# Two transformer layers on one Trainium2 core: attention values issued in the same stretch as a score visit

## The chip, the core and the metric

The kernel runs on one core of a Trainium2 chip. The metric is device time in microseconds (us) of one execution; a run is given as the median over several executions. The names of the engines are those of the profile: PE is TensorE (matmul), PEld its weight loads, ACT is ScalarE, DVE is VectorE, POOL is GpSimd, SP is SyncE, which here only issues DMA transfers.

## What is computed

Two layers, one after the other, each an attention block and a gated MLP, both on the normalized residual stream. The second layer has the same weights.

```python
x = A_x                                   # 1 x 2048 x 512, bf16
for _ in range(2):
    x = x + attention(layernorm(x))       # 32 heads of 16, each query sees itself and the 255 keys before it
    x = x + mlp(layernorm(x))             # (sigmoid(x Wg) * (x Wu)) Wd, hidden width 1792
# attention: softmax(q k^T / 4, masked) v, then Wo; q, k, v = x Wqkv
```

## The kernel before

The 2048 rows are 16 tiles of 128 (`t`), in four groups of four (`g`); `L` is the layer. All engines' programs are written by a planner that runs while the program is built: the class `Plan` keeps an assumed clock for each engine, tasks for ACT, DVE, POOL and SP enter queues with a priority (a lower number goes first), and `pick` (from line 1024) decides what PE gets next whenever the assumed PE is free. What comes out is a fixed order of instructions for each engine, with semaphores between them. So the times in the planner (such as `EXP_NS = 1880`) order the instructions, and the chip then runs that order as fast as its waits allow.

PE's work has three kinds. The planner calls them modes, since the array is used in three shapes:

- "d", full 128x128 matmuls: units for q, k and v (L572, L601, L637), gate and up (L662), down (L695), output projection (L723), a few transposes through PE (L532, L999), and matmuls on the identity that fill empty time in the first 85 us of the plan (L1108, `keep_warm`). Each unit writes one of four PSUM banks (`bank`), and the bank is given back when ACT or DVE has copied it out.
- "s", score visits (L853, L863, L873): 24 to 32 small matmuls in strips of 32 rows that fill the tile `Sps`, which takes four PSUM banks and exists once. After each visit ACT makes one exponential of 128x2048 (L905) into the ring `PTring` or into `edge`, and only then may the next visit overwrite `Sps`. A tile has five visits (one "R", four "A"), the last tile of a layer two; that is 154 visits. A visit is due when `PACE` has passed since the one before (2700 ns in the first layer, 3000 ns in the second) and its exponential is planned to be over.
- "pv", values (L932): for each half of the heads of a tile, 32 to 80 small matmuls in strips of 32 columns into one bank. They need the exponentials and the masks that DVE multiplies into them (L791), the values `Vaug` (copied out of PSUM by ACT or DVE, L553 or L555), and copies of every second row of them, `Vl` and `Vh`, which SP's DMA makes (L1131). There are 64.

After the values: the bank is copied to `OTs` by ACT (L553) or DVE (L555), whichever is planned to be done first; then a DMA transpose to `Oq` (L951), the division by the softmax sum on DVE (`norm`, L986 and L987), a DMA transpose to `OnT` (L959), the output projection on PE, the sum and the layer norm on DVE and POOL (L729, L498 to L520), a DMA transpose to `xnT` (L544), gate and up for a tile or a pair of tiles, tanh on ACT (L674), the product into `hT` on DVE (L677), and the down projection (L695, L704).

In `pick`, `go` is the time until the exponential of the last visit is over, `wait` the longer of that and of what is left of the pace. In the kernel before, values that are ready go when the next visit is due within 600 ns (or when no visit is in sight, or when the last exponential has not begun):

```python
if pv and (wait <= 600 or wait > 1e8 or held):
    return self.do_values(pv, spare)
```

Of the kernel before, what the change touches and what calls it, by code (L numbers as in the profile page):

```python
# [15 lines left out]
NT = S // P  # L16
# [8 lines left out]
NBG = TGW // P  # L25
# [58 lines left out]
def dve_ns(n):  # L84
    return 152 + n / 0.96
# [43 lines left out]
def when_all(events, fn):  # L129
    left = [e for e in events if not e.fired]  # L130
    if not left:
        fn()
        return
    count = [len(left)]

    def one():
        count[0] -= 1
        if count[0] == 0:
            fn()

    for e in left:
        e.waiting.append(one)
# [152 lines left out]
def mm_ns(n):  # L295
    return n / 2.4 + 2.5


class Net:
# [74 lines left out]
    def loads(self, A_x, wqkv, wo, w_gate, w_up, w_down):  # L374
        nc, pl = self.nc, self.pl
        wq_src = wqkv.rearrange("(k p) m -> p k m", p=P)
        wo_src = wo.rearrange("(k p) m -> p k m", p=P)
        wd_src = w_down.rearrange("(c p) m -> p c m", p=P)
        wg_src = w_gate.rearrange("(k p) f -> p k f", p=P)
        wu_src = w_up.rearrange("(k p) f -> p k f", p=P)  # L380
        self.has_x, self.has_wq = {}, {}

        def load_x(dst, tiles, n, prio, queues=("SP", "SP"), after=0):
            done, parts = Event(), []
            for z in range(2):
                src = A_x[0].rearrange("(t z k) d -> z k t d", z=2, k=HP)[z][:, tiles, :]
                parts.append(load(dst[z:P:2], src, n * HP * D * 2, after, (), prio, queues[z]))
            when_all(parts, done.fire)
            return done

        def load(dst, src, nbytes, after=0, deps=(), prio=2, queue="SP"):
            ns = max(520, 40 + nbytes / 1024 * 0.95)
            q = {"SP": nc.sync, "ACT": nc.scalar}[queue]
            return pl.dma(ns, nbytes, lambda: q.dma_start(out=dst, in_=src), deps, prio, after, queue).done

        for t in range(0, NBG, 2):
            self.has_x[t] = self.has_x[t + 1] = load_x(self.xsb[:, t:t + 2, :], slice(t, t + 2), 2, 0, ("SP", "ACT"))
        for i, k in enumerate("kqv"):
            h = slice("qkv".index(k) * D, ("qkv".index(k) + 1) * D)
            self.has_wq[k] = load(self.wq[:, :, h], wq_src[:, :, h], D * D * 2, prio=0, queue="ACT" if i < 3 else "SP")  # L400

        def x_group(g, after):
            h = slice(g * NBG, (g + 1) * NBG)
            ev = load_x(self.xsb[:, h, :], h, NBG, 2 if g > 1 else 2, after=after)
            for t in range(g * NBG, (g + 1) * NBG):
                self.has_x[t] = ev

        x_group(1, 0)
        gap, at = 1300, 6000
        self.has_wo = load(self.wot[:], wo_src, D * D * 2, after=at)  # L410
        at += gap * 2
        n = F // 2
        gu = []
        for i in range(2):
            h = slice(i * n, (i + 1) * n)
            pair = []
            for w, src in ((self.wg, wg_src), (self.wu, wu_src)):
                pair.append(load(w[:, :, h], src[:, :, h], D * n * 2, after=at))
                at += gap * 7 // 2
            gu.append(pair)  # L420
            if i == 0:
                x_group(2, at)
                at += gap * 2
        self.has_gu = [gu[fc * 2 // FC] for fc in range(FC)]
        self.has_wd = Event()
        parts = []
        for i in range(0, FC, 2):
            h = slice(i, i + 2)
            parts.append(load(self.wd[:, h, :], wd_src[:, h, :], 2 * P * D * 2, after=at))
            at += gap  # L430
        when_all(parts, self.has_wd.fire)
        x_group(3, at)
# [257 lines left out]
    def down_unit(self, L, t, t0, n, chunks):  # L690
        nc, pl = self.nc, self.pl

        def mm(bank, fc):
            c, o = (chunks[fc], (t - t0) * P) if n == 2 else (chunks[fc // 2], fc % 2 * P)
            nc.tensor.matmul(self.banks[bank][:], lhsT=self.hT[:, c, o:o + P], rhs=self.wd[:, fc, :],  # L695
                             start=fc == 0, stop=fc == FC - 1)
            if t == t0 + n - 1:
                pl.at(pl.pe_free + PE_LATENCY, self.h_used[L, t0, fc].fire)

        def steps(bank):  # L700
            return [(mm_ns(D), lambda fc=fc: mm(bank, fc)) for fc in range(FC)]

        def evac(u):
            d = pl.task({"DVE": dve_ns(D)}, lambda e: nc.vector.scalar_tensor_tensor(  # L704
                out=self.xsb[:, t, :], in0=self.banks[u.bank][:], scalar=0.5, in1=self.xsb[:, t, :],
                op0=ALU.mult, op1=ALU.add), [u.done], 1)
            if L == 0:
                self.layer_norm(("p", 1, t // NBG), t, [d.done], 5)
            else:
                dst = self.out[0, t * P:(t + 1) * P, :].rearrange("(z k) d -> z k d", z=2)  # L710
                for z in range(2):
                    pl.dma(450, HP * D * 2, lambda z=z: nc.sync.dma_start(out=dst[z], in_=self.xsb[z:P:2, t, :]), [d.done])
            return d.done

        u = Unit(("d", L, t), steps, [self.has_wd] + ([] if t == t0 else [self.down_began[L, t - 1]]), False, evac)
        u.want = [self.h_ready[L, t0, fc] for fc in range(FC)]
        return u

    def oproj_unit(self, L, t, b):
        nc, pl = self.nc, self.pl  # L720

        def steps(bank):
            return [(mm_ns(D), lambda c=c: nc.tensor.matmul(  # L723
                self.banks[bank][:], lhsT=b[0][:, c, :], rhs=self.wot[:, c, :],
                start=c == 0, stop=c == KT - 1)) for c in range(KT)]

        def evac(u):
            u.done.then(lambda: self.give(b))
            d = pl.task({"DVE": dve_ns(D)}, lambda e: nc.vector.tensor_tensor(  # L729
                out=self.xsb[:, t, :], in0=self.xsb[:, t, :], in1=self.banks[u.bank][:], op=ALU.add), [u.done], 1)  # L730
            self.layer_norm(("g", L, t // NBG), t, [d.done], 0 if L * NT + t < 1 else 2)
            return d.done

        return Unit(("o", L, t), steps, [self.has_wo], False, evac)
# [203 lines left out]
    def after_values(self, L, t, half, bank, done):  # L938
        nc, pl = self.nc, self.pl
        box = self.outs.setdefault((L, t), {})  # L940
        early = L * NT + t < 1

        def move(e):
            if "OTs" not in box:
# [24 lines left out]
        b = pl.dma(1800, 262144, turn, [box[0], box[1]], 0 if early else 1)  # L969
        b.can = lambda: self.has("Oq")  # L970
        b.done.then(lambda: self.give(box["OTs"]))
        c = pl.task({"DVE": 960}, norm, [b.done], 0 if early else 3, lambda: self.has("On"), port=True)
        c.done.then(lambda: (self.give(box["Oq"]), self.give(box["Rt"])))
        d = pl.dma(1190, 131072, turn2, [c.done], 0 if early else 1)
        d.can = lambda: self.has("OnT")
# [53 lines left out]
    def pick(self):  # L1029

        pl = self.pl
        s = self.slot
        visit = None
        wait = 1e9
        if s < len(self.visits):
            if s == 0 or self.exps[s - 1].ends is not None:
                if all(e.fired for e in self.v_needs[s]):
                    wait = 0 if s == 0 or self.exps[s - 1].done.fired else self.exps[s - 1].ends - pl.now
                    visit = self.visits[s]
            elif all(e.fired for e in self.v_needs[s]):  # L1040
                wait = EXP_NS
        go = wait
        wait = max(wait, self.last_s + self.pace(s) - pl.now)
        pv = None
        spare = [i for i in range(BANKS) if self.bank_user[i] is None]
        if self.pv_list and spare:
            L, t, h = self.pv_list[0]
            if len(self.masks[L, t, h]) == self.n_masks(t) and all(e.fired for e in self.masks[L, t, h]) and all(
                    self.v_ready[L, jj].fired for jj in range(max(0, t - 2), t + 1)) and self.v_lo[L, t].fired and (
                    t < 2 or self.v_hi[L, t - 2].fired):  # L1050
                pv = self.pv_list[0]
        held = s < len(self.visits) and s > 0 and self.exps[s - 1].ends is None
        if pv and (wait <= 600 or wait > 1e8 or held):
            return self.do_values(pv, spare)
        u = None
        if wait >= 60:
# [1 line left out]
        if visit and (wait <= 0 or go <= 0 and u is None):  # L1058
# [4 lines left out]
            L, t = visit[:2]  # L1063
# [166 lines left out]
    def go(self, *srcs):  # L1230
        pl = self.pl
# [45 lines left out]
        c = 0  # L1277
        for L in range(2):
            t0 = 0
            while t0 < NT:  # L1280
                k = 1 if L * NT + t0 < 4 or L * NT + t0 >= 2 * NT - 0 else 2
                m = FC * k // 2
                chunks = [(c + i) % HCH for i in range(m)]
                c += m
                gs += [self.gate_up_unit(L, t0, k, (i,) if k == 2 else (2 * i, 2 * i + 1), chunks[i]) for i in range(m)]
                for t in range(t0, t0 + k):
                    d = self.down_unit(L, t, t0, k, chunks)
                    d.begin = self.down_began[L, t]
                    ds.append(d)
                t0 += k  # L1290
# [51 lines left out]
```

## Time and profile before

| | |
|---|---|
| median of 6 runs | 554.66 us (553.48 to 556.49) |
| the profiled execution | 554.57 us, of which the span from the first to the last instruction is 552.8 us |
| PE, PEld, ACT, DVE, POOL busy | 537.1, 353.8, 411.2, 397.9, 62.3 us |
| exponentials (L905 on ACT, `PTring` and `edge`) | 122 of 1853 ns and 32 of 1774 ns in the mean |
| gate and up matmuls (L662) | 1568 with 256 columns, 448 with 128 |
| copies to `OTs` | 39 on ACT, 25 on DVE |

An engine is busy from the start of an instruction to its end; the ends of matmuls are modelled and overlap the next start, so matmuls are better read by the distance of their starts. "Idle before" is the idle time of an engine ahead of an instruction, and the name behind the arrow is what ended it. The chain is followed back from the last instruction to whatever released each step. The profiled execution is 0.09 us under the median, and 1.77 us of it lie outside the span.

### The profile page before, as it was taken

Reading aid. Unit: us, or ns where it says so; the run is one execution under the profiler, and the core shown is the slowest. Engines: PE = TensorE matmul, PEld = TensorE weight load, DVE = VectorE, ACT = ScalarE, POOL = GpSimd, SP = SyncE. Lnnn points to the kernel's source line nnn. Section 1 sums busy time; section 2 is a strip of 40 time slices with the busy share of each in tenths; the row PEclk is TensorE's granted clock in tenths of the full one; section 3 lists DMA queues with packets and bytes.
Section 4 is the critical chain, followed back from the end, with each engine's and each line's share of the span. In section 5 each row is a group of like instructions: output and inputs, shape, how many; then the busy total and the mean of one; then the engine's idle time right before and its main releaser. Section 6 shows DMA issues by size and latency. Waiting matters only on the chain.

```text
span 552.8 us, 24052 instructions
## 1 busy us (share of the span) xinstructions
PE 537.1 (97%) x10848; PEld 353.8 (64%) x10848; DVE 397.9 (72%) x879; ACT 411.2 (74%) x486; POOL 62.3 (11%) x145
## 2 busy tenths in 40 slices
PE   7999998999999999999999999999999999999997
PEld 6447756756657665665666756666666756666773
DVE  6989777887779769769676687667666685766432
ACT  3799888889978888688687876978869778753321
POOL 5212011111011111102100031000000000000000
PEclk9999999999999999999999999999999999999999
DMA  8693532142315222234301143022530332223100
GB/s 276 219 223 81 61 52 42 33 60 45 59 36 95 41 61 42 52 51 88 69 12 41 42 79 71 17 46 54 92 74 17 46 69 61 48 53 54 24 20 30
DMA packets 97015, 36.41 MB, mean 66 GB/s; under 512 B 79248, under 2 KB 96912, under 8 KB 96912
## 3 DMA queue, kind: packets, MB, share of 16 engines
q1 hardware_dynamic: 95040, 33.04, 29.5%
q8 instruction: 85, 1.39, 1.0%
q10 hardware_dynamic: 1872, 1.84, 1.0%
q14 instruction: 18, 0.15, 0.1%
HBM read 9.70 MB, written 2.10 MB: 21 GB/s over the span
## 4 chain that ended last, share of the span: by engine, by line
PE 85%; DVE 6%; ACT 4%; DMA 3%; issue 1%; SPq 0%; ACTq 0%; DVEq 0%
PE bank L662 32%; PE bank L695 17%; PE bank L932 8%; PE Sps L853 6%; PE bank L723 5%; PE bank L572 5%; PE bank L637 4%; PE bank L601 4%; ACT PTring L905 3%; DMA OnT<-On 3%; PE Sps L863 2%; DVE PTring L791 1%; DVE st L498 1%; DVE kTp L615 1%; DVE xsb L704 0%
## 5 line engine op out<-in xcount | busy, mean ns | idle before, releaser
L905 ACT ACTIVATE PTring<-Sps 128x2048 bf16<-128x2048 f32 (+1 forms) x122 | 226.0, 1853 | 33.3 <-PE Sps L853 30.9
L662 PE MATMUL bank<-xnT,wg 128*128 128x256 bf16 (+1 forms) x1008 | 141.3, 261 | 0.8 <-DVE Rt L986 0.8
L662 PE MATMUL bank<-xnT,wu 128*128 128x256 bf16 (+1 forms) x1008 | 139.5, 261 | 0.0
L677 DVE SCALAR_TENSOR_TENSOR hT<-th,bank 128x256 bf16<-128x256 bf16 x224 | 87.4, 414 | 41.2 <-ACT th L674 40.7
L674 ACT ACTIVATE th<-bank 128x256 bf16<-128x256 f32 x224 | 80.5, 388 | 48.3 <-PE bank L662 44.8
L695 PE MATMUL bank<-wd,hT 128*128 128x512 bf16 x448 | 113.7, 380 | 0.0
L662 PEld LDWEIGHTS <-wg 128*128 128x128 bf16 x1008 | 87.0, 98 | 27.3 <-issue 2.0
L662 PEld LDWEIGHTS <-wu 128*128 128x128 bf16 x1008 | 89.8, 98 | 13.5 <-issue 1.4
L791 DVE TENSOR_TENSOR PTring<-PTring,mask 128x1024 bf16<-128x1024 bf16 x64 | 44.0, 687 | 42.9 <-ACT PTring L905 42.7
L503 POOL TENSOR_SCALAR st<-st 128x1 f32<-128x1 f32 x64 | 19.3, 301 | 446.2 <-DVE st L499 446.2
L695 PEld LDWEIGHTS <-hT 128*128 128x128 bf16 x448 | 41.3, 98 | 36.4 <-issue 1.8
L905 ACT ACTIVATE edge<-Sps 128x2048 bf16<-128x2048 f32 (+1 forms) x32 | 56.8, 1774 | 7.5 <-PE Sps L863 7.0
L932 PEld LDWEIGHTS <-Vaug 128*32 128x32 bf16 x2880 | 44.3, 97 | 15.4 <-issue 13.1
L932 PE MATMUL bank<-PTring,Vaug 128*32 128x64 bf16 (+1 forms) x2880 | 52.4, 203 | 0.5 <-DVE PTring L791 0.3
L853 PE MATMUL Sps<-qT,kTp 32*128 32x64 bf16 (+3 forms) x1856 | 48.3, 218 | 2.0 <-ACT PTring L905 1.0
L553 ACT CAST OTs<-bank 128x512 bf16<-128x512 f32 x39 | 28.9, 740 | 22.9 <-PE bank L932 22.1
L853 PEld LDWEIGHTS <-kTp 32*128 32x128 bf16 x1856 | 24.9, 92 | 31.2 <-issue 28.0
L932 PE MATMUL bank<-edge,Vl 128*32 128x64 bf16 x1024 | 44.4, 193 | 0.0
L498 DVE BATCH_NORM_STATS2 st<-xsb 128x6 f32<-128x512 bf16 x64 | 43.7, 683 | 0.5
L791 DVE TENSOR_TENSOR edge<-edge,maske 128x1024 bf16<-128x1024 bf16 x60 | 40.2, 682 | 1.1 <-ACT edge L905 1.1
L932 PE MATMUL bank<-edge,Vh 128*32 128x64 bf16 x896 | 40.8, 193 | 0.0
L504 POOL TENSOR_TENSOR st<-st,nhalf 128x1 f32<-128x1 f32 x64 | 39.6, 618 | 5.3
(72 smaller groups left out, 544.3 us busy)
## 6 DMA issues: line engine op xcount, KB each, us to landing
Vl<-Vaug SPq DMA_DIRECT2D x32, 68.0 KB, 2.4
out_dram<-xsb SPq DMA_DIRECT2D x32, 64.0 KB, 1.9
Vh<-Vaug SPq DMA_DIRECT2D x28, 68.0 KB, 2.5
wg<-in_B_w_gate_dram SPq DMA_DIRECT2D x2, 896.0 KB, 12.2
wu<-in_B_w_up_dram SPq DMA_DIRECT2D x2, 896.0 KB, 5.3
wd<-in_B_w_down_dram SPq DMA_DIRECT2D x7, 256.0 KB, 4.4
wq<-in_A_wqkv_dram ACTq DMA_DIRECT2D x3, 512.0 KB, 6.9
xsb<-in_A_x_dram SPq DMA_DIRECT2D x6, 256.0 KB, 8.5
```

The costliest lines, as they stand in the source:

```text
L498: nc.vector.bn_stats(out=st[:, 0:6], in_=self.xsb[:, t, :])
L504: nc.gpsimd.tensor_tensor(out=st[:, 8:9], in0=st[:, 9:10], in1=self.nhalf[:], op=ALU.pow)
L553: self.nc.scalar.copy(out=out, in_=in_)
L572: return [(mm_ns(w), lambda kt=kt, o=o: nc.tensor.matmul(self.banks[bank][:, o:o + w], lhsT=self.wq[:, kt, cq * P:cq * P + P], rhs=self.xn ...
L662: return [(mm_ns(w), lambda i=i, j=j, fc=fc, wt=wt, kt=kt: nc.tensor.matmul(pt[:, i, j, :], lhsT=wt[:, kt, fc * P:(fc + 1) * P], rhs=self. ...
L674: nc.scalar.activation(out=box["th"][0][:], in_=pt[:, 0, :], func=AF.Tanh, scale=0.5)
L677: nc.vector.scalar_tensor_tensor(out=self.hT[:, chunk, :], in0=box["th"][0][:], scalar=1.0, in1=pt[:, 1, :], op0=ALU.add, op1=ALU.mult)
L695: nc.tensor.matmul(self.banks[bank][:], lhsT=self.hT[:, c, o:o + P], rhs=self.wd[:, fc, :], start=fc == 0, stop=fc == FC - 1)
L791: done = pl.task({"DVE": dve_bf_ns(1024)}, lambda e: nc.vector.tensor_tensor(out=r, in0=r, in1=m.to_broadcast([P, 16, HP]), op=ALU.mult), ...
L853: nc.tensor.matmul(self.sps[:, m, o:o + n * HP], lhsT=kTp[32 * m:32 * m + 32, i, tt, e, :], rhs=self.qT[32 * m:32 * m + 32, i, q0:q0 + n * ...
L905: nc.scalar.activation(out=out, in_=src, func=AF.Exp, scale=scale)
L932: nc.tensor.matmul(o, lhsT=Va[:, c0:c0 + 32], rhs=p(h), start=k == 0 or t == 0, stop=k == len(parts) - 1 or t == 0, tile_position=(0, 32 * g))
```

## The change

The rule for values in `pick` is rewritten. Values that are ready now go when PE is not in mode "d": directly behind a visit, or behind other values. In mode "d" they go only when the visit is overdue (`wait <= -1`), when no visit is in sight, or when the last exponential has not begun. And when PE has just done values and the exponential before is over, the next visit follows at once, whatever is left of its pace. Six constants change with it: the spacing of the weight loads, four priorities, and the last four tiles of the second layer go through gate and up one by one and not in pairs.

```diff
@@ loads
-        gap, at = 1300, 6000
+        gap, at = 1600, 6000
@@ down_unit
-                self.layer_norm(("p", 1, t // NBG), t, [d.done], 5)
+                self.layer_norm(("p", 1, t // NBG), t, [d.done], 3)
@@ oproj_unit
-            self.layer_norm(("g", L, t // NBG), t, [d.done], 0 if L * NT + t < 1 else 2)
+            self.layer_norm(("g", L, t // NBG), t, [d.done], 1 if L * NT + t < 4 else 2)
@@ after_values
-        early = L * NT + t < 1
+        early = L * NT + t < 4
...
-        c = pl.task({"DVE": 960}, norm, [b.done], 0 if early else 3, lambda: self.has("On"), port=True)
+        c = pl.task({"DVE": 960}, norm, [b.done], 0 if early else 2, lambda: self.has("On"), port=True)
@@ pick
         held = s < len(self.visits) and s > 0 and self.exps[s - 1].ends is None
-        if pv and (wait <= 600 or wait > 1e8 or held):
+        if visit and pl.mode == "pv" and go <= 0:
+            if go > 0:
+                return False
+            wait = go
+        elif pv and (pl.mode != "d" and 1 or wait <= -1 or wait > 1e8 or held):
             return self.do_values(pv, spare)
         u = None
         if wait >= 60:
@@ go
-                k = 1 if L * NT + t0 < 4 or L * NT + t0 >= 2 * NT - 0 else 2
+                k = 1 if L * NT + t0 < 4 or L * NT + t0 >= 2 * NT - 4 else 2
```

## The prediction

> **What bounds the kernel now.** I read the page first: which engine is full.
>
> ```profile
> PE 537.1 (97%) x10848; PEld 353.8 (64%) x10848; DVE 397.9 (72%) x879; ACT 411.2 (74%) x486; POOL 62.3 (11%) x145
> PEclk9999999999999999999999999999999999999999
> ```
>
> PE is busy 97% of the span at full clock; ACT and DVE are not full. So the time is PE's own work plus the places where PE waits. Then the list of waits, for PE's rows and for those of ACT and DVE that this change can touch (total us, times, longest):
>
> ```profile
> DVE hT L677 <- ACT th L674: 40.7, 59, 2.2
> ACT PTring L905 <- PE Sps L853: 30.9, 49, 1.7
> ACT OTs L553 <- PE bank L932: 22.1, 31, 1.8
> ...
> ACT Vaug L553 <- DMA Vl<-Vaug: 3.0, 1, 3.0
> ...
> PE bank L723 <- DMA OnT<-On: 2.0, 3, 0.7
> ...
> PE Sps L863 <- ACT PTring L905: 1.3, 2, 0.7
> ...
> PE bank L572 <- ACT Vaug L553: 1.1, 1, 1.1
> ...
> PE Sps L853 <- ACT PTring L905: 1.0, 2, 0.8
> ```
>
> The long rows belong to engines that have time to spare. PE's rows are short: about 5.4 us in these four. One ACT row stands out, a single wait of 3.0 us. The timelines of ACT and PE there (start, length, what, idle before):
>
> ```profile
> 21.69 1.89 ACT L905 ACTIVATE edge<-Sps 128x2048 bf16<-128x2048 f32 x1
> 26.55 0.59 ACT L553 CAST Vaug<-bank 128x512 bf16<-128x512 f32 x1 [2.98 <-DMA Vl<-Vaug]
> 27.04 1.88 ACT L905 ACTIVATE PTring<-Sps 128x2048 bf16<-128x2048 f32 x1
> ```
>
> ```profile
> 24.59 1.46 PE L637 MATMUL bank<-wq,xnT 128*128 128x512 bf16 x6
> 27.19 1.02 PE L572 MATMUL bank<-xnT,wq 128*128 128x512 bf16 x4 [1.15 <-ACT Vaug L553]
> 28.97 0.41 PE L853 MATMUL Sps<-qT,kTp 32*128 32x128 bf16 x24 [0.75 <-ACT PTring L905]
> ```
>
> ACT must copy values into `Vaug` and waits until the DMA that reads that tile has landed. The exponential queued behind the copy (its visit began on PE at 24.02) starts at 27.04; PE loses 1.15 us for the bank and 0.75 us at the next visit.
>
> Last, the chain, for the price of matmuls (start, us, what, count):
>
> ```profile
> 51.98 1.00 PE bank L1108 x16
> ...
> 67.61 0.89 PE bank L662 x16
> ...
> 531.71 1.75 PE bank L662 x16
> ...
> 542.17 6.49 PE bank L695 x30
> ```
>
> 16 gate/up matmuls of 128 columns take 0.89 us (55.6 ns each), 16 of 256 columns 1.75 us (109.4 ns). At the end PE runs without a gap to its last down matmul.
>
> **The change part by part.** Both programs have a fixed order for each engine, so I compare the orders.
>
> *The tie.* A stretch of tiled work (visit or values between full matmuls) was 102 times a visit alone, 30 values then visit, 21 visit then values, 12 others: 165. In the new order it is 99 visits alone, 52 visit then values, 3 the other way, 9 values alone: 163. So the tie turns the pairs round and hardly makes new ones. Entering tiled work costs 0.21 us (the weight loads' idle time before values at 240.94 and before the visit at 244.93), leaving it 0.13 to 0.16 us (242.82 to 242.98), a change inside about 0.14 us (241.61 to 241.75). Two stretches fewer, two inner changes more (53 to 55): -2 x 0.34 + 2 x 0.14 = **-0.4 us**.
>
> *The values move behind the visit.* Adding row durations along PE's orders, values start 0.5 us later after their visit in the first layer (4.7 to 5.3 us in the mean), 0.3 us in the second. Waiting for them are the `OTs` copy and, on ACT, the exponential that overwrites their scores; tanh and copies are queued behind that. From values to the visit of that exponential at least 2.0 us are left (3.5 before), so it does not wait: 0. PE's own waits for masks (L932 for L791, 0.5 us on the page) came where 2.4 to 2.8 us lay between visit and values; now the least is 2.8: **-0.3** (-0.5 to +0.5).
>
> *Waits at visits.* Start to start a visit needs about 0.45 us until its exponential begins, 1.88 us of it and 0.05: 2.4 us. Adding rows along PE's order, the shortfalls add up to 1.8 us before and 2.35 us after (ten short places for six): **+0.5** (0 to +1.2).
>
> *The copies.* With the visit first, ACT is in an exponential when the values end, so 26 `OTs` copies go to DVE (ACT 39 to 13, DVE 25 to 51). ACT loses 26 x 0.736 = 19.1 us, DVE gains 26 x 0.728 = 18.9 us (72% to 75%). Exponentials directly behind such a copy on ACT fall from 29 to 6; each began some 0.3 us late, which cost PE only where the next visit was close. DVE's copies are covered by its idle time, 40.7 us before `hT` alone: **0**; without that cover, see the second rival. [...]
>
> *The wait at 24 us.* In the new order the six copies from the first `Vaug` to `Vl` and `Vh` stand together on SP, and this ACT copy waits for PE alone. It can then run at 23.58, its exponential at about 24.5 and not 27.04, and PE's next two steps find bank and `Sps` free: **-1.9 us** (0 if the next wait swallows it). The cause is the shift of SP's order, which the larger spacing of the weight loads helps to make.
>
> *Filling matmuls.* L1108 falls from 104 to 84: 20 x 1.00/16 = **-1.2 us** (0 if only idle time takes their place).
>
> *Single tiles at the end.* 224 matmuls of 256 columns become 448 of 128: 448 x 55.6 - 224 x 109.4 = 24.9 - 24.5 = **+0.4 us**; evacuations keep their size (two halves of a bank), and PE has no gap in this stage. [...]
>
> *Output projections and first gates.* PE waits 2.0 us for `OnT` (L723). From the second values to the output projection the shortest distances on PE's order are 10.4, 10.5, 10.8 us before and 9.8, 10.5, 10.6 after, while the projections that stalled had needed 11 to 13: **+0.5** (-0.5 to +1.5). From projection to first gate PE needs 7.4 to 7.8 us without a stall; one distance shrinks to 7.1, others grow to 9.7 and more: 0 (-0.8 to +0.8). The division on DVE and the layer norms move up a little in DVE's queue; masks and products behind them wait at most one step (0.35 + 0.69 us), covered as above: 0.
>
> *Loads.* The last `wd` load is planned some 7 us later (24 steps of 0.3), and the second half of `wu` stands behind six copies on SP and not two. That load was issued at 25.00, the last of `wd` by 39.3, and they land in 5.3 and 4.4 us (page, medians); gate and up begin at 46.5, the first down matmul is at 59.4: hidden by 8 us and more, 0.
>
> Sum: -0.4 - 0.3 + 0.5 - 1.9 - 1.2 + 0.4 + 0.5 = **-2.4 us**. The profiled execution was 554.57 us (552.8 of span and 1.8 outside it), 0.1 under the median: 554.57 - 2.4 = 552.2, and with the median 552.3. About 0.3% (1.7 us) is what a measurement of this kernel can tell from no change, so this is just beyond it.
>
> **The rivals.**
>
> *Nothing measurable (0.23).* The change does not do what its name says: 163 stretches for 165. Without the -1.9 (ACT begins earlier, only to meet the next wait) or the -1.2, the sum is -0.5 to -1.2: about 553.8. For it: a new order brings waits of its own, and PE waited some 15 us in all. Against it: the copy at 24 us has no DMA to wait for.
>
> *Slower: DVE (0.22).* 26 copies of 0.73 us enter DVE's in-order queue, between scores and masks, products and sums. A `hT` product or an evacuation behind one is up to 0.73 us late, its bank comes back late, and PE, with four banks, waits. A hit in a third of the places costs 9 x 0.7 = 6.3 us less the 2.4 above: about 558; from six hits on, the gain is gone and more (4.1 us turn -2.4 into +1.7). For it: slices with DVE at 9 tenths in the first layer. Against it: DVE sits idle 40.7 us for tanh and PE waits for DVE hardly anywhere now.
>
> *More (part of faster, 0.08).* The exponentials lead by 2.5 us from 24 us on, and in the first 85 us PE was filled with L1108 for want of work; if that lead is kept and the waits at visits and for `OnT` vanish too (4.4 us without the 0.75 counted, half of them say), it is about 550.
>
> **How the numbers follow.** Forecast -2.4 us with 0.47, more with 0.08: faster than 553.0 with 0.55. Within 0.3%, 0.23; above 556.3, 0.22. The uncertain terms reach from about -3.5 to +1.5 together; the range goes from 549.2 (the "more" case with room) to 557.2, which takes in half of the slower case and leaves out about 0.17. The likeliest case's own range is 550.5 to 553.0.
>
> **What would show it.** Right: ACT has no wait for `Vl` near 24 us, and PE no gap of 1.15 at the q unit nor of 0.75 at the visit after it; L1108 84 times; L662 with 128 columns still 0.89 us for 16; OTs 13 on ACT, 51 on DVE; PE's busy time nearly the same and its idle time some 2 us less. Wrong: PE rows that wait for `hT`, `xsb` or other DVE work in the list of waits, longer idle time before L723 or L853, or a gap before the last down matmuls.

## The result, and the profile after

The changed kernel takes 552.03 us (median of 36 executions, 550.71 to 555.53); the kernel before, on the same chip, 554.37 us (78 executions). The ratio is 0.9963 with an interval of 0.9955 to 0.9971: 2.05 us less, 1.6 to 2.5 by the interval (the two medians differ by 2.34). The prediction was 552.3.

The page of the changed kernel, PE's line of the busy times and the row of its instruction queue q8 (packets, MB, share):

```profile
PE 537.1 (97%) x11052; PEld 355.4 (64%) x11052; DVE 413.2 (75%) x901; ACT 398.7 (72%) x464; POOL 62.0 (11%) x145
q8 instruction: 86, 1.41, 1.0%
```

PE is busy for 537.1 us, as before to the tenth; its idle time, the rest of the span, falls from 15.7 to 15.1 us, and not by the 2 us that the prediction named as a sign of being right. DVE and ACT have changed places (75% and 72%). Then the list of waits, the rows that answer to those shown before, and all of PE's rows of 0.7 us and more that belong to the stages after the first:

```profile
ACT PTring L905 <- PE Sps L853: 47.0, 76, 1.7
DVE hT L677 <- ACT th L674: 41.7, 53, 3.6
...
ACT OTs L553 <- PE bank L932: 7.8, 6, 2.6
...
PE bank L932 <- issue: 1.9, 1, 1.9
PE bank L723 <- DMA OnT<-On: 1.6, 4, 0.6
...
PE Sps L853 <- ACT PTring L905: 1.2, 4, 0.4
...
PE bank L572 <- DVE hT L677: 0.8, 1, 0.8
...
PE bank L662 <- issue: 0.7, 1, 0.7
```

The row of ACT that waited 3.0 us for the DMA from `Vaug` to `Vl` is gone, and so is PE's row for that bank. ACT now waits 47 us for visits (30.9 before): it is further ahead of PE. PE's waits behind "issue", which the list of waits cannot put down to anything, have grown: 1.9 and 0.7 us here, one of 0.8 us before. The timelines of ACT and PE at 24 us (start, length, what, idle before):

```profile
21.69 1.89 ACT L905 ACTIVATE edge<-Sps 128x2048 bf16<-128x2048 f32 x1
23.69 0.59 ACT L553 CAST Vaug<-bank 128x512 bf16<-128x512 f32 x1
24.49 1.88 ACT L905 ACTIVATE PTring<-Sps 128x2048 bf16<-128x2048 f32 x1 [0.21 <-PE Sps L853]
```

```profile
24.59 1.46 PE L637 MATMUL bank<-wq,xnT 128*128 128x512 bf16 x6
25.89 1.03 PE L572 MATMUL bank<-xnT,wq 128*128 128x512 bf16 x4
26.85 0.41 PE L853 MATMUL Sps<-qT,kTp 32*128 32x128 bf16 x24
```

Both traces have the v unit at 24.59. Before, the q unit followed at 27.19 and the visit at 28.97; now at 25.89 and 26.85. That is 2.12 us at one place, about as much as the whole change gains. At the end of the chain:

```profile
510.02 0.89 PE bank L662 x16
...
540.55 0.89 PE bank L662 x16
541.45 6.71 PE bank L695 x31
```

The narrow gate and up matmuls cost 55.6 ns each here too, and PE has no gap to the end.

One place got worse. PE in the values of the last tile, and the clock granted there (columns of the second: us, PE, PEld, DVE, ACT and POOL busy, PEclk, DMA share, GB/s):

```profile
493.17 0.20 PE L932 MATMUL bank<-edge,Vl 128*32 128x64 bf16 x2
495.27 0.21 PE L932 MATMUL bank<-edge,Vl 128*32 128x64 bf16 x2 [1.91 <-issue]
```

```profile
492.00:496.00 4.00, 2.10 (x104) 1.62 (x93) 1.03 (x3) 1.24 (x2) 0.00 (x0) 1.00 0.20 41
496.30:499.70 3.40, 3.40 (x19) 2.34 (x17) 0.84 (x2) 1.07 (x3) 0.00 (x0) 0.50 0.42 82
```

PE stands still for 1.91 us in the middle of a row of equal matmuls, and the clock is then at half for 3.4 us, in which PE is busy all the time. Four gate and up matmuls of 256 columns take 0.86 us there (496.46 to 497.32) and 0.44 us after it (501.11 to 501.55): by that an estimated 1.7 us more. The profiled execution is 553.97 us (552.2 of span), 1.94 over its median and only 0.6 under the profiled execution before.

### The profile page after: what moved, and what is told of

It reads as the page before. It is cut to its first block, busy times and chain, and to the rows that moved or that the text cites. A ratio compares the mean times of both kernels' runs of the same rounds, so it can differ in the third digit from the quotient of the medians.

```text
span 552.2 us, 24438 instructions
## 1 busy us (share of the span) xinstructions
PE 537.1 (97%) x11052; PEld 355.4 (64%) x11052; DVE 413.2 (75%) x901; ACT 398.7 (72%) x464; POOL 62.0 (11%) x145
## 4 chain that ended last, share of the span: by engine, by line
PE 89%; DMA 4%; DVE 3%; ACT 2%; issue 1%
PE bank L662 34%; PE bank L695 17%; PE bank L932 8%; PE Sps L853 7%; PE bank L723 5%; PE bank L572 5%; PE bank L601 5%; PE bank L637 5%; DMA OnT<-On 3%; PE Sps L863 2%; ACT PTring L905 2%; DVE st L498 1%; DMA Oq<-OTs 1%; DVE On L987 0%; PE bank L532 0%
## 5 line engine op out<-in xcount | busy, mean ns | idle before, releaser
L695 PE MATMUL bank<-wd,hT 128*128 128x512 bf16 x448 | 115.7, 380 | 0.0
L662 PEld LDWEIGHTS <-wg 128*128 128x128 bf16 x1120 | 90.8, 98 | 27.1 <-issue 2.2
L662 PEld LDWEIGHTS <-wu 128*128 128x128 bf16 x1120 | 92.5, 98 | 12.7 <-issue 1.5
L791 DVE TENSOR_TENSOR PTring<-PTring,mask 128x1024 bf16<-128x1024 bf16 x64 | 44.0, 687 | 30.8 <-ACT PTring L905 30.5
L932 PE MATMUL bank<-PTring,Vaug 128*32 128x64 bf16 (+1 forms) x2880 | 52.2, 203 | 0.0
L932 PEld LDWEIGHTS <-Vaug 128*32 128x32 bf16 x2880 | 44.1, 97 | 10.1 <-issue 6.8
L853 PEld LDWEIGHTS <-kTp 32*128 32x128 bf16 x1856 | 24.9, 92 | 39.0 <-issue 36.9
L853 PE MATMUL Sps<-qT,kTp 32*128 32x64 bf16 (+3 forms) x1856 | 48.0, 218 | 1.6 <-ACT PTring L905 1.2
L932 PE MATMUL bank<-edge,Vl 128*32 128x64 bf16 x1024 | 44.9, 193 | 1.9 <-issue 1.9
L791 DVE TENSOR_TENSOR edge<-edge,maske 128x1024 bf16<-128x1024 bf16 x60 | 40.5, 684 | 4.9 <-ACT edge L905 4.8
L555 DVE CAST OTs<-bank 128x512 bf16<-128x512 f32 x51 | 37.2, 730 | 7.5 <-PE bank L932 7.0
L932 PE MATMUL bank<-edge,Vh 128*32 128x64 bf16 x896 | 40.9, 193 | 0.0
```

Of the source, the lines that this page charges most:

```text
L555: self.nc.vector.tensor_copy(out=out, in_=in_)
L662: return [(mm_ns(w), lambda i=i, j=j, fc=fc, wt=wt, kt=kt: nc.tensor.matmul(pt[:, i, j, :], lhsT=wt[:, kt, fc * P:(fc + 1) * P], rhs=self. ...
L791: done = pl.task({"DVE": dve_bf_ns(1024)}, lambda e: nc.vector.tensor_tensor(out=r, in0=r, in1=m.to_broadcast([P, 16, HP]), op=ALU.mult), ...
L853: nc.tensor.matmul(self.sps[:, m, o:o + n * HP], lhsT=kTp[32 * m:32 * m + 32, i, tt, e, :], rhs=self.qT[32 * m:32 * m + 32, i, q0:q0 + n * ...
L932: nc.tensor.matmul(o, lhsT=Va[:, c0:c0 + 32], rhs=p(h), start=k == 0 or t == 0, stop=k == len(parts) - 1 or t == 0, tile_position=(0, 32 * g))
```

## The experiments

Three groups ran, each on a chip of its own; the kernel before had 555.87, 555.18 and 555.65 us there, so times are read as ratios to it. The ratios and their intervals (in brackets) are those of the record; the quotient of two medians can differ from them by up to 0.0025. "Before plus" and "changed kernel with" name what each kernel starts from.

**b_split: before plus `Vaug` in halves.** The DMA that holds the copy at 24 us reads other key tiles of `Vaug` than the copy writes. Here each buffer is two tiles, and the order of work on PE, ACT and SP stays.

```diff
-self.Vaug = [big.tile([P, NBG, VW], ...) for i in range(3)]
+self.Vaug = [[big.tile([P, 2, VW], ...) for k in range(NBG // 2)] for i in range(3)]
...
-dst = self.Vaug[gi % 3][:, t % NBG, ...]
+dst = self.Vaug[gi % 3][t % NBG // 2][:, t % 2, ...]
```

> The kernel before, with each Vaug buffer split into two tiles of two key tiles each (six more small memsets on DVE, everything else in the same order on every engine). The ACT copy at 26.55 us then has no DMA of another key tile to wait for; nothing else changes. Theory 'wait at 24 us': ACT's 2.98 us wait and PE's gaps of 1.15 and 0.75 us go, and the time falls by 1.9 us to about 552.5 (ratio 0.9966). Theory 'tie' (the gain comes from the rule for values): no change, 554.4 (1.000).

Measured: 553.45 us, 0.9952 [0.9929, 0.9975]. ACT and PE around the copy (this execution ran at half clock from 10.9 to 14.4 us, 0.51 in the mean, and all stands 1.6 us later):

```profile
25.30 0.59 ACT L553 CAST Vaug0b<-bank 128x512 bf16<-128x512 f32 x1
26.09 1.88 ACT L905 ACTIVATE PTring<-Sps 128x2048 bf16<-128x2048 f32 x1 [0.20 <-PE Sps L853]
```

```profile
26.20 1.46 PE L637 MATMUL bank<-wq,xnT 128*128 128x512 bf16 x6
27.49 1.03 PE L572 MATMUL bank<-xnT,wq 128*128 128x512 bf16 x4
28.45 0.41 PE L853 MATMUL Sps<-qT,kTp 32*128 32x128 bf16 x24
```

The wait is gone, and q unit and visit follow the v unit at the distances of the changed kernel. So it never was a wait for data: the semaphore stood for the whole buffer. Taking it away alone, with the old rule and the old constants, gives 1.4 to 3.9 us. The 1.9 of the prediction lies inside. The size comes from the medians: the profiled execution took 555.53 us, 2.1 over its median, and has one wait of 1.78 us for `OnT` at 320 us that the trace before has not.

**b_gap, b_tie, a_gap, a_oldrule: which part takes the wait away.** The first two put one part of the change into the kernel before, the other two take it out of the changed kernel.

```diff
# b_gap (before), and the reverse in a_gap (changed kernel)
-        gap, at = 1300, 6000
+        gap, at = 1600, 6000
# b_tie (before), and the reverse in a_oldrule (changed kernel)
-        if pv and (wait <= 600 or wait > 1e8 or held):
+        if visit and pl.mode == "pv" and go <= 0:
...
+        elif pv and (pl.mode != "d" and 1 or wait <= -1 or wait > 1e8 or held):
```

> The kernel before with only the spacing of the weight loads at 1600 instead of 1300. On SP the first copies to Vl then come after the ACT copy in program order, so that copy waits for PE alone. Theory 'wait at 24 us': -1.9 us, about 552.5 (0.9966), give or take 0.7 for what the new order does elsewhere. Theory 'tie': 554.4 (1.000).

Measured: 556.02 us, 0.9989 [0.9968, 1.0011]. The wait at 24 us is gone, as expected, but hardly anything is left of the gain. In the order that the new spacing makes, two visits wait for the exponentials before them:

```profile
129.28 0.41 PE L853 MATMUL Sps<-qT,kTp 32*128 32x64 bf16 x24 [1.50 <-ACT PTring L905]
...
131.73 0.61 PE L853 MATMUL Sps<-qT,kTp 32*128 32x64 bf16 x24 [0.74 <-ACT PTring L905]
132.28 4.02 PE L601 MATMUL bank<-xnT,wq 128*128 128x512 bf16 x9
```

```profile
132.50:135.80 3.30, 3.30 (x9) 1.16 (x8) 1.57 (x4) 1.83 (x1) 0.00 (x0) 0.50 0.34 20
```

That is 2.2 us of waits, as much as the spacing saves at 24 us. In this execution the clock is also at half from 130.4 to 137.2 us (its nine matmuls of L601 take 4.02 us, the six of L637 in b_split 1.46), an estimated 3.0 us more; but it took 557.99 us, 2.0 over the median, and has the lowest mean clock of the twelve (0.991; the median is 0.996), so the others need not have it. By the ratio the spacing alone gains 0.6 us (-0.6 to +1.8): not to be told from nothing, and the 1.9 is just outside.

> The kernel before with only the new rule for values and visits in pick; all constants as before. The wait of ACT for Vl stays in the program. Theory 'wait at 24 us': the ACT wait of about 3 us and PE's gaps are still there, and the time is 553.8 (0.999; what is left of the sum without the 1.9). Theory 'tie': 552.3 (0.9963), with or without the wait.

Measured: 556.1 us, 0.9994 [0.9973, 1.0016]. The rule alone gives nothing that can be measured, and the wait stands as before:

```profile
ACT Vaug L553 <- DMA Vl<-Vaug: 3.0, 1, 3.0
```

Its trace has one kind of wait in the place of another. Counting waits of PE of 0.2 us or more after the first 20 us, those with a known releaser fall from 6.5 us (kernel before) to 3.8, and those behind "issue" grow from 0.8 to 3.4 us.

> The changed kernel with the spacing of the weight loads put back to 1300. The wait of ACT for Vl is back in the program. Theory 'wait at 24 us': +1.9 us on the changed kernel, about 554.0 (0.9995 of the kernel before). Theory 'tie': 552.0 (0.9963), as the changed kernel.

Measured: 558.08 us, 1.0034 [1.0008, 1.0061]. The wait is back on ACT and on PE:

```profile
27.38 0.59 ACT L553 CAST Vaug<-bank 128x512 bf16<-128x512 f32 x1 [2.99 <-DMA Vl<-Vaug]
```

```profile
28.02 1.02 PE L572 MATMUL bank<-xnT,wq 128*128 128x512 bf16 x4 [1.16 <-ACT Vaug L553]
29.79 0.61 PE L853 MATMUL Sps<-qT,kTp 32*128 32x128 bf16 x24 [0.75 <-ACT PTring L905]
```

Against the ratio of the changed kernel this is 0.7% more (3.9 us), twice the 1.9. The trace shows two things beside the wait itself: the granted clock is 0.50 from 29.8 to 33.1 us, an estimated 1.7 us as in the changed kernel, and the "issue" waits are 0.46, 1.74 and 1.40 us, 3.6 in all (2.9 in the changed kernel). How much of this the other executions have is not known.

> The changed kernel with the old rule for values put back in pick, all six constants as changed. ACT's copy has no DMA to wait for. Theory 'wait at 24 us' with the sum of the prediction: the 2 us at 24 us are kept, the rule is worth little, 0.996 to 0.999. Theory 'tie': 1.000 or slower. The spacing alone, on the kernel before, gave 0.9989 since it made new waits at 127 to 131 us; if the rule's part is to avoid such waits, this run is near 0.999 too and has waits at visits again.

Measured: 552.61 us, 0.9940 [0.9912, 0.9968]: with the old rule and the six new constants it is as fast as with the new rule. So the part of the change that carries its name is worth nothing that can be measured, from either side. The gain comes with the constants, and among them the spacing is the one that moves SP's copies to `Vl`. The spacing is needed (a_gap) but not enough by itself (b_gap); which of the other five constants it needs beside it, no run shows. The old rule has 1.2 us of PE's waits for masks (L932 for L791) in its trace, the changed kernel none.

**a_split: the changed kernel with `Vaug` in halves.** The edit is that of b_split.

> The changed kernel with Vaug split into tiles of two key tiles. There the copy at 24 us has no DMA to wait for already, so theory 'wait at 24 us' expects no change against the changed kernel, 0.996. If copies of values wait for other DMAs unseen, it is faster than that by more than 0.2%. The profile also shows whether PE's wait of 1.91 us at 493 us that nothing in the profile explains belongs to the order (then it is there again) or to that one execution.

Measured: 552.66 us, 0.9934 [0.9907, 0.9960]. That is 0.3% under the ratio of the changed kernel, which was taken on another chip, and the two intervals touch; a_oldrule, without the split, has 0.9940 on this chip. So no second gain of b_split's size can be told: what the split takes away was already gone. The wait at 493 us that the expectation asks about is there again: 1.50 us at 494.3, behind "issue". So it belongs to the order and not to one execution.

**a_ots_act and b_ots_dve: who copies to `OTs`.** PE's order stays, all 64 copies go to one engine.

```diff
# a_ots_act (changed kernel); "DVE" in b_ots_dve (before)
-            self.copy(e, box["OTs"][0][:, 4 * half...
+            self.copy("ACT", box["OTs"][0][:, 4 * half...
```

> The changed kernel, PE's order untouched, with all 64 copies to OTs on ACT (51 come back from DVE). A copy behind its visit's exponential is up to 1.9 us late, and holds a PSUM bank as long. My term: the moved copies were the right ones to move, so this is slower than the changed kernel by 1 to 4 us, 0.998 to 1.003. Rival 'DVE becomes the bound': faster than the changed kernel, under 0.994.

Measured: 559.1 us, 1.0056 [1.0029, 1.0082], 6.4 us more than a_split on the same chip. PE now waits for these copies:

```profile
PE bank L723 <- ACT OTs L553: 1.4, 3, 0.8
...
PE bank L662 <- ACT OTs L553: 1.2, 3, 0.7
PE bank L1112 <- ACT OTs L553: 1.0, 2, 0.8
```

> The kernel before, PE's order untouched, with all 64 copies to OTs on DVE (39 come over from ACT). My term for the copies: DVE has room, exponentials behind a copy begin 0.3 us earlier, waits at visits shrink by some 0.5 us: 0.999. Rival 'DVE becomes the bound': 39 copies of 0.73 us in DVE's queue make banks late, 1.005 to 1.011, with PE waiting for DVE rows.

Measured: 557.82 us, 1.0023 [0.9993, 1.0054]: not to be told from no change. PE waits for DVE in it where the rival said (0.9 us once for `hT`, 0.7 us for masks), but not often. So 39 more copies on DVE cost 0.5% at most (by the interval), and 51 more on ACT cost about 1%. No run moves only the 26 that the change moves.

**b_nofill and a_nofill: the filling matmuls.** The prediction counted 20 fewer of them as 1.2 us. Here those after the first 20 us of the plan are left out and the planned time is kept, so the order of all other work stays: 44 fewer in the kernel before, 24 fewer in the changed one.

```diff
 def keep_warm(self, bank):
-        for i in range(4):
+        for i in range(4 if pl.now < 20000 else 0):
```

> The kernel before without the 44 matmuls on the identity that stand after the first 20 us of the plan (104 become 60); every other instruction in the same order. My term 'filling matmuls cost their time': 44 x 62 ns = -2.7 us, 0.995. Rival 'they only fill idle time': PE waits at the next unit instead, 0 to -0.5 us, 0.999 to 1.000. Rival 'they keep the clock up': PE's clock is halved for a stretch between 37 and 60 us, and the time is 1 to 2 us longer, 1.002 to 1.004.

Measured: 557.45 us, 1.0033 [1.0018, 1.0048]: slower, though 44 x 1.00/16 = 2.75 us of PE's work are gone. PE's waits over 0.2 us after the first 20 us, added up in the trace, go from 7.3 to 11.3 us. 4.0 us more of waits and 2.75 us less of work make 1.25 us, near the 1.8 measured. Among the rows that grew or are new:

```profile
PE bank L723 <- DMA OnT<-On: 2.1, 2, 1.1
PE bank L932 <- issue: 1.8, 2, 1.0
...
PE bank L662 <- DVE hT L677: 1.0, 2, 0.7
```

The clock stays full to the end of PE's work (0.999 in the mean of the profiled execution), so the filling does not earn its place by keeping the clock up. All other matmuls stand in the same order in both traces and can be laid over each other: the run without the filling is never more than 1.3 us ahead, and behind from 250 us on. So the time that is freed early goes into waits.

> The changed kernel without the 24 matmuls on the identity that stand after the first 20 us of the plan (84 become 60). 'They cost their time': 24 x 62 ns = -1.5 us on the changed kernel, 0.9936 of the kernel before. 'They only fill': 0.996. 'They keep the clock up': 0.998 or more.

Measured: 548.71 us, 0.9877 [0.9856, 0.9898], faster than both kernels. The same edit goes the other way: PE's waits fall from 6.6 to 3.7 us, the 1.91 us at 495 and the half clock behind it are gone:

```profile
PE Sps L853 <- ACT PTring L905: 1.2, 4, 0.4
PE bank L662 <- issue: 1.0, 2, 0.5
```

The spans of the two profiled executions differ by 5.3 us (552.2 and 546.9). Laid over the changed kernel matmul by matmul, this run is within 1.0 us of it up to 380 us, though all 24 matmuls were to stand between 32 and 58 us: the 1.5 us of work are not what it gains. It is 1.4 us ahead at 422 us, where the waits for `OnT` (1.1 us) are gone, 1.6 at 479, and 5.3 behind the place at 495.

**a_pairs: the last four tiles in pairs again.**

```diff
-                k = 1 if L * NT + t0 < 4 or L * NT + t0 >= 2 * NT - 4 else 2
+                k = 1 if L * NT + t0 < 4 or L * NT + t0 >= 2 * NT - 0 else 2
```

> The changed kernel with the last four tiles of the second layer in pairs again (224 gate and up matmuls of 256 columns in the place of 448 of 128). My term: -0.4 us on the changed kernel, 0.9956. [...] If single tiles at the end save a wait that I did not see, it is slower than the changed kernel, 0.998 or more.

Measured: 552.43 us, 0.9942 [0.9922, 0.9963]. Nothing here tells single tiles from pairs (the changed kernel has 0.9963, on another chip).

**a_space_nofill: a_nofill with the last two values kept apart.** After the last visit values wait until 5 us of the plan have passed since the values before.

```diff
-        elif pv and (... or wait > 1e8 or held):
+        elif pv and (... or wait > 1e8 and (s < len(self.visits) or pl.now - self.last_pv > 5000) or held):
```

> The changed kernel without the 24 filling matmuls and with the last values of the last tile kept apart from the values before them (about 2 us of gate and up between them, and not 0.3). In the traces of the changed kernel and of its variants PE waits 1.4 to 1.9 us at 493 us, in the second of two values that stand close together, for nothing that the profile shows. If two values in close succession outrun what brings PE its instructions, the wait goes and this is 1.5 us under the run without the filling matmuls alone; if the wait belongs to that point of the program, it stays and the two runs agree.

Measured: 550.08 us, 0.9896 [0.9874, 0.9919]. The intervals of the two overlap: no gain, since a_nofill no longer has the wait that the spacing was to take away. So this run does not decide what that wait was.

## Why the prediction was right, and where it was not

**The wait at 24 us (-1.9).** Right in place, size and cause. The rows show 2.12 us at the visit, b_split shows 2.7 us (1.4 to 3.9) for the wait alone, and a_gap brings it back. In b_gap the wait goes too, but new waits take the gain: the prediction's bracket "0 if the next wait swallows it". What the prediction did not have: the copy and the DMA touch different key tiles, so the data never asked for the wait.

**The tie (-0.4).** Right that it hardly makes pairs that were not there. b_tie and a_oldrule give it nothing measurable from both sides; the price of -0.4 itself is too small for any run.

**The copies (0).** Right, as far as the runs tell: with all 64 on ACT (51 moved back) the kernel loses 6.4 us, and with all 64 on DVE nothing that can be measured. With 51 of 64 on DVE (see the rows) DVE is at 75% and PE waits once for `hT`, 0.8 us.

```profile
L555 DVE CAST OTs<-bank x51: 696/732/745, 30.6 to 485.7; 128x512 bf16<-128x512 f32 x51
...
L553 ACT CAST OTs<-bank x13: 730/736/755, 33.5 to 495.5; 128x512 bf16<-128x512 f32 x13
```

**The filling matmuls (-1.2): the term that does not hold.** The count fell from 104 to 84, but "so many matmuls fewer times their duration" is not what such an edit is worth. Taking out 44 cost 1.8 us in one order, taking out 24 gained about 0.8 to 0.9% in the other. The traces laid over each other show why: the freed time is gone into waits within the next stages, which is the prediction's own bracket, "0 if only idle time takes their place". Both differences are what the edit does to waits elsewhere.

**Visits and output projections (+0.5 and +0.5).** Wrong in sign. Without the 0.75 already counted, the rows for visits go from 1.55 to 1.2 us (L863 and L853 for ACT), those for `OnT` from 2.0 to 1.6. ACT's lead from 24 us on, which the prediction put into the case "more", is a possible reason; no run separates it. The waits for masks went from 0.3 to none on the list (predicted -0.3), and one of 0.8 us for `Rt` on DVE went with them, while the one of 0.8 us for `hT` is new.

**Single tiles (+0.4).** The price of 0.89 us for 16 was right; a_pairs cannot resolve the rest.

**What the sum did not have.** The "issue" waits on PE grew from 0.8 to 2.9 us (0.34, 0.68 and 1.91), with an estimated 1.7 us for the 3.41 us of half clock behind the last. With the waits as the two traces have them, and the tie, the filling and the single tiles as the prediction priced them, the sum is -0.4 - 0.3 - 0.35 - 1.9 - 1.2 + 0.4 - 0.4 = -4.15, with these waits about -2.0, and with the half clock about -0.35. The two profiled executions differ by 0.6, all executions by 2.05 in the ratio. (PE's waits in the first 20 us, 3.5 us before and 4.3 after, are in neither sum; they are 3.5 again in a_nofill, which has the same order there.) Of the other executions only the mean clock is known: 17 had 0.999 or more, with a median of 551.77 us, and 19 had less, with 552.94. So the number was met with some luck, because two errors cancel: PE's ordinary waits went better than predicted, and a kind of wait that the prediction had not looked at went worse.

**The rivals.** "Nothing measurable" is out only just: the gain is 1.6 to 2.5 us, and the prediction called 1.7 us the least that can be told. Its argument, that the change does not do what its name says, was right (b_tie, a_oldrule). "Slower: DVE" falls with the waits and with b_ots_dve, where 64 copies on DVE cost 0.5% at most. "More" was not reached by this change; a_nofill, by another way, is there.

## What to carry to other kernels

A wait for a DMA on a buffer that holds several tiles may be one for the buffer and not for the data: see which part each side touches, and split the buffer before reordering anything. Ask of every row in a list of waits what is queued behind it: one 3.0 us wait on an engine with a quarter of its time free was worth more (b_split, 0.9952) than the new rule for all 64 values (b_tie, 0.9994). And when an order written by a planner changes, compare the sums of PE's waits over several variants before giving one edit the credit: the same deletion cost 0.3% in one order and gained close to 1% in the other.

## What the runs showed of the hardware

**The "issue" waits and the packets of q8.** The "issue" waits are not scattered. PE's program is 21,696 weight loads and matmuls before and 22,104 after, and the page has 85 and 86 packets of 16.4 KB in the instruction queue q8: one for every 255 and every 257 of them. Ten traces, all of which have every matmul's record, have 28 waits of 0.2 us or more behind "issue" after the first 20 us. All 28 stand before the instruction at place 194 or 195 modulo 256 of PE's program, which counts its semaphore instructions too; a block, here, is the 256 instructions from one such place to the next. The trace also has the packets' times: each of the 28 waits ends 2.2 to 3.0 us after a packet has begun (the one at 495.27 after a packet from 492.60 to 493.87), and, with the packets put to the blocks in their order, in the ten traces no block's first instruction runs sooner than 2.2 us after its packet's begin. The packet of the next block begins, in the median, 0.8 us after PE has begun the block it is in. A block takes 5.9 us in the median of these kernels. But the 78 values matmuls from 492.50 to 493.17 take 0.7 us, 8.8 ns each: at that rate, an estimate, 128 pairs of them take about 1.1 us. Of the eight waits of 0.9 us and more, seven follow a block with 120 to 128 values matmuls among its 128, the eighth one with 80. Three blocks with 114 to 117 (before, b_split, b_gap, at about 500 us) have no wait behind them. What ends these waits is not shown: the traces have places and times alone.

An edit far away moves the boundaries of the blocks. In a_nofill PE's order at this place is the same, but 24 pairs fewer lie ahead, the block ends among gate and up matmuls, and PE runs through:

```profile
491.59 0.21 PE L932 MATMUL bank<-edge,Vl 128*32 128x64 bf16 x4
491.73 0.28 PE L662 MATMUL bank<-xnT,wg 128*128 128x256 bf16 x1
491.85 0.60 PE L662 MATMUL bank<-xnT,wu 128*128 128x256 bf16 x4
```

Whether tying values to visits costs more of these waits is not shown: b_tie has 3.4 us of them and the kernel before 0.8, but a_oldrule, without the tie, has 2.9, as has the changed kernel. Over the ten traces there are 28 waits at some 850 boundaries, of up to 1.9 us. That these boundaries make most of a_nofill's gain is the author's reading of the two traces (3.8 of the 5.3 us arise at 495 us, wait and half clock together); no run moved the boundaries and nothing else.

**The clock after small gaps.** It fell to half for 3.41 us behind 1.91 us of idle PE in the changed kernel and behind 1.16 and 0.75 us in a_gap, and for 6.83 us behind 1.50 us in b_gap, where the wait of 0.74 us lies inside. In the changed kernel PE was busy for 2.10 of the 4.00 us from 492.00 to 496.00 (the row with the result), and the fall is at 496.32.

The same gaps of 1.15 and 0.75 us left the clock full in the kernel before. The traces show one difference. The falls of one execution lie whole multiples of 3.413 us apart (496.32 and 550.94 us in the changed kernel are 16 of them, 9.25 and 29.73 us in a_gap are 6). Counted in stretches of that length from the falls, the two gaps of a_gap lie in the stretch that ends at 29.73 us, with 1.85 us of idle PE; in the kernel before, counted back from the fall at 552.66 us, a stretch ends at 27.01 us and divides them into 0.96 and 0.94 us. What decides between the two cases is not shown: a stretch with 1.59 us of idle PE (b_gap) was followed by a fall, and the wait of 1.78 us in b_split, at 320 us, was not (its mean clock of 0.997 is what the 3.5 us at 10.9 us alone make).
